# Order of two steps in the opening of a gated attention and expert-mix kernel: POOL's sums of x behind the low part of the score weights, a load of x behind a load of score weights

## The chip, the cores and the metric

The kernel runs on one core of a Trainium2 chip. Five engines work side by side, each through its own list of instructions in order, and wait for one another by semaphores: PE (matrix products), DVE and POOL (elementwise work and sums), ACT (copies, casts and functions such as exp), and SP, which here only issues DMA transfers. The metric is the device time of one execution in microseconds (us). Before the change it was 379.66 us, the median of three runs (379.59 to 382.38).

## The reference, cut to what matters

```python
g = sigmoid((x * gate_w).sum(-1, keepdims=True))
# a: linear attention with a learned feature map, 32 heads of 16
q, k, v = split_heads(x @ wqkv)
phi = lambda p: concat(softmax(p @ w_phi), softmax(-(p @ w_phi)))
kv, z = phi(k).T @ v, phi(k).sum(over tokens)
a = (phi(q) @ kv) / (phi(q) @ z + 1e-6) @ wo
# b: per token and head the best of 16 x 16 experts
s1, s2 = (x @ w_q)[first half] @ k1.T, (x @ w_q)[second half] @ k2.T
e = argmax(s1) * 16 + argmax(s2)
b = sum over heads of gelu(x . u[e]) * v[e]
return g * a + (1 - g) * b
```

x has 2048 rows of 512 numbers, so 16 tiles of 128 rows; all is float32.

## The kernel before, in words

A float32 product is made of three faster ones: each operand is split into a high part (a cast, written by ACT or DVE) and a low part (the rest, written by DVE or POOL), and PE adds high by high, high by low and low by high. So each operand has a pair of tiles: `xh` and `xl` for x, `sh` and `sl` for the score weights, `gh` and `gl` for sums of x.

The kernel has two large stages. The first (until about 118 us) reads x and makes the keys and values of all tiles, adds up `kv`, and beside that builds the score weights. The second goes over the 16 tiles once more for queries, scores and the output. The change lies in the first stage, which is written out by hand: the order of the lines is the order in which each engine gets its work.

Opening loop (lines 418 to 456), t = 0 to 4. For each t: keys of tile t (`kproj`, `k_diffs`, `k_exp`, `k_sum`, `k_mult`), one or more steps of `score`, and the split of a later tile of x (`x_split(t + 3)` at line 435).

Block-pair loop (lines 471 to 553), t = 5, 7, 9, 11, 13. Tiles t and n = t + 1 are taken together: their keys and values come from seven block products instead of eight (`prod`, line 461), which need sums and differences of the two raw tiles of x. The keys of tile n are finished in the next pass (`behind`). This text calls these passes "pass 5", "pass 7" and so on.

- `x_load(t)` (line 149): SP issues the DMA of a raw tile of x, 256 KB, into one of four buffers `xr`. In the opening loop, at lines 419 and 420, tile 7 is loaded at t = 1 and tile 8 at t = 2, ahead of the other work of that t. Tile 8 takes the buffer of tile 4, so its DMA waits until `x_split(4)` is done.
- `load_wq()` (line 143, called from `score`, line 406): SP issues the DMA of a block of `w_q`, 1 MB, into one of two buffers `st`. Block 4 takes the buffer of block 2, so its DMA waits until PE has used block 2 (`score_w`, line 299).
- `score` (line 400): PE multiplies a block of `w_q` by the keys k1 or k2 (`score_w`). After two blocks, `score_planes` (line 302) has ACT copy the result out of PSUM as 16-bit halves (`wpl`, line 304) and SP issue a DMA transposition of it (`wtp`, line 306).
- `join_tp` (line 314) has ACT put the transposed halves together again in the one buffer `wtj`; `join_end` (line 318) has ACT cast this to `sh` (line 321) and POOL write the rest to `sl` (line 322). Since `wtj` has one buffer, the next `join_tp` waits for that POOL instruction.
- `Sums.add(t)` (lines 172 to 178): four POOL instructions that replace raw tiles t and t + 1 by their sums and differences in place. They wait until the raw tiles have been split (`x_low`, line 156, on DVE). `Sums.high` (ACT, line 183) and `Sums.low` (POOL or DVE, line 189) split these sums for the products of the next pass.

In pass 5 POOL's list is: `Sums.add(7)`, the `sl` of column block 1 (`join_end(j1, tj1)`, line 500), `k_mult(4)` (line 516), the `sl` of column block 2 (from `join_all`, line 517), two small memsets, `Sums.low(7)`, `k_mult(5)`. ACT's list in pass 5 is: copy `pu` (489), `wtj` 1 (496), `wpl` 2 (497), `sh` 1, copy `pv` (512), exp of tile 4 (514), `wtj` 2, `sh` 2, `wpl` 3 (from `score`), `v` (531), exp of tile 5 (532), copy `pk` (536), and then `Sums.high(7)`. PE's last products of pass 5 (line 543) need that copy `pk`.

## Time and profile before

| | |
|---|---|
| median of three runs | 379.66 us (379.59 to 382.38) |
| the profiled execution, its time | 379.46 us |
| its span, first to last instruction | 376.8 us |
| granted PE clock, mean over the span | 0.994 |
| busy share of PE, DVE, ACT, POOL | 97%, 88%, 67%, 54% |
| wq loads, median from issue to landing | 6.2 us, 1024 KB each, 16 of them |
| transpositions `wtp`, median from issue to landing | 6.3 us, 8 of them |

In the views quoted below, times are us from the span's start. A timeline row has start, length, engine, line of the kernel, operation and tiles; a bracket gives the idle time of the engine before it and what ended that. The chain of work is followed back from the last instruction and lists, in order of time, what each moment waited for. A wait is a pair of who waited and for whom, with total, count and longest. A stretch gives the busy time of each engine between two times, the granted clock, and the DMA's share and rate. Lines of DMA issues give the queue, the count, the size and the time from issue to landing.

### The profile page before, as it was taken

How to read it: one execution, taken by the hardware profiler on the slowest of the kernel's cores; microseconds unless marked ns; L12 is line 12 of the kernel's file. 1: busy time of each engine (PE TensorE's matmuls, PEld its weight loads, DVE VectorE, ACT ScalarE, POOL GpSimd, SP SyncE). 2: the span in 40 equal slices, each digit the busy share in tenths (PEclk: the TensorE clock that was granted, in tenths of full speed). 3: DMA queues.
4: the chain of work that ended last, by engine and by line, in shares of the span. 5: the costliest groups of instructions: out<-in, count | busy, mean ns of one | idle time of the engine just before them, and what ended most of it. 6: DMA issues, size and time to landing. Idle time of an engine off the chain costs nothing.

```text
span 376.8 us, 8980 instructions
## 1 busy us (share of the span) xinstructions
PE 366.5 (97%) x3519; PEld 289.0 (77%) x3519; DVE 332.3 (88%) x783; ACT 253.0 (67%) x449; POOL 203.9 (54%) x205
## 2 busy tenths in 40 slices
PE   7999996999999999999999999999999999999996
PEld 3766675778778888878888888888888888888775
DVE  4679886999968889999999999899999999999993
ACT  4585657766766454879668678686686686687741
POOL 1089987698838726646427436344454454464700
PEclk9999998999999999999999999999999999999999
DMA  7867995359665032363342461453532532623201
GB/s 264 323 237 257 223 324 184 145 193 298 231 178 83 3 86 83 59 99 81 75 97 66 90 98 46 85 110 31 113 67 68 118 61 67 128 52 76 68 32 56
DMA packets 72219, 46.67 MB, mean 124 GB/s; under 512 B 63601, under 2 KB 64497, under 8 KB 69873
## 3 DMA queue, kind: packets, MB, share of 16 engines
q1 hardware_dynamic: 71312, 45.24, 45.8%
q10 hardware_dynamic: 864, 0.87, 0.8%
q8 instruction: 27, 0.44, 0.5%
q14 instruction: 16, 0.12, 0.1%
HBM read 26.43 MB, written 4.19 MB: 81 GB/s over the span
## 4 chain that ended last, share of the span: by engine, by line
PE 85%; DVE 4%; POOL 3%; ACT 3%; issue 2%; DMA 2%; SPq 0%; POOLq 0%; ACTq 0%; DVEq 0%
PE po L863 11%; PE s L56 8%; PE s L57 8%; PE s L58 8%; PE po L870 5%; PE pk L461 5%; PE pq L56 5%; PE pq L58 4%; PE pq L57 4%; PE pu L461 3%; PE oT L751 3%; PE pp L57 2%; PE pp L58 2%; PE pp L56 2%; PE ws L299 2%; PE kvacc L283 2%
## 5 line engine op out<-in xcount | busy, mean ns | idle before, releaser
L665 POOL TENSOR_TENSOR w<-d,zb 128x512 f32<-128x512 f32 x32 | 41.2, 1305 | 78.1 <-ACT d L659 78.1
L56 PE MATMUL s<-sh,xh 128*128 128x512 f32 x128 | 50.9, 398 | 0.0
L57 PE MATMUL s<-sl,xh 128*128 128x512 f32 x128 | 49.9, 390 | 0.0
L58 PE MATMUL s<-sh,xl 128*128 128x512 f32 x128 | 49.8, 389 | 0.0
L700 POOL TENSOR_TENSOR d<-d,st 128x512 f32<-128x512 f32 x30 | 31.2, 1063 | 27.7 <-DVE st L694 25.5
L659 ACT ACTIVATE d<-d 128x512 f32<-128x512 f32 x32 | 20.1, 632 | 34.7 <-DVE d L119 26.6
L276 POOL TENSOR_TENSOR d<-d,st 128x1024 f32<-128x1024 f32 x16 | 33.9, 2117 | 14.3 <-ACT d L267 10.0
L742 ACT COPY pt<-tp 128x1024 uint16<-128x1024 uint16 x28 | 36.3, 1364 | 0.0
L732 ACT COPY pl<-d 128x1024 uint16<-128x1024 uint16 x28 | 29.2, 1044 | 6.7 <-POOL d L700 6.7
L58 PEld LDWEIGHTS s<-sh,xl 128*128 128x128 f32 x128 | 24.0, 188 | 5.1
L56 PEld LDWEIGHTS s<-sh,xh 128*128 128x128 f32 x128 | 24.0, 188 | 4.7
L57 PEld LDWEIGHTS s<-sl,xh 128*128 128x128 f32 x128 | 24.1, 188 | 4.6
L56 PE MATMUL pq<-wah,xh 128*128 128x512 f32 x64 | 26.8, 418 | 0.0
L271 DVE TENSOR_REDUCE st<-d 128x64 f32<-128x1024 f32 x16 | 19.5, 1216 | 8.1 <-ACT d L267 7.7
L58 PE MATMUL pq<-wah,xl 128*128 128x512 f32 x64 | 25.1, 392 | 0.0
L57 PE MATMUL pq<-wal,xh 128*128 128x512 f32 x64 | 25.0, 390 | 0.0
L669 DVE TENSOR_REDUCE st<-d 128x32 f32<-128x512 f32 x32 | 21.6, 682 | 1.9 <-ACT d L659 0.4
L709 DVE TENSOR_TENSOR eq<-s,mx 128x512 bf16<-128x512 f32 x32 | 22.1, 691 | 1.2
L708 DVE TENSOR_REDUCE mx<-s 128x32 f32<-128x512 f32 x32 | 21.7, 680 | 0.0
L156 DVE TENSOR_TENSOR xl<-xr,xh 128x512 fp32r<-128x512 f32 (+2 forms) x17 | 19.1, 1149 | 1.8 <-ACT xh L152 1.6
L679 DVE TENSOR_REDUCE st<-w 128x32 f32<-128x512 f32 x32 | 20.4, 675 | 0.1
L267 ACT ACTIVATE d<-d 128x1024 f32<-128x1024 f32 x16 | 17.0, 1064 | 3.5 <-DVE d L121 3.5
(253 smaller groups left out, 1117.2 us busy)
## 6 DMA issues: line engine op xcount, KB each, us to landing
wq<-wq SPq DMA_DIRECT2D x16, 1024.0 KB, 6.2
xr<-xT SPq DMA_DIRECT2D x15, 256.0 KB, 4.7
y<-ot SPq DMA_DIRECT2D x15, 256.0 KB, 2.4
rawk<-wkT SPq DMA_DIRECT2D x1, 1024.0 KB, 6.6
rawq<-wqT SPq DMA_DIRECT2D x1, 1024.0 KB, 7.1
rawo<-wo SPq DMA_DIRECT2D x4, 256.0 KB, 3.6
rawu<-ug SPq DMA_DIRECT2D x2, 258.0 KB, 3.7
rawv<-wv ACTq DMA_DIRECT2D x2, 256.0 KB, 4.6
```

The source lines that it names most:

```text
L56: pe.matmul(o, ah, bh, start=(first and i == 0), stop=False)
L57: pe.matmul(o, ah, bl, start=False, stop=False)
L58: pe.matmul(o, al, bh, start=False, stop=(last and i == n - 1))
L276: pool.tensor_tensor(g64(d), g64(d), b64(st[:, 128:192]), op=ALU.mult)
L461: pe.matmul(o, x_, w_, start=(first and i + j == 0), stop=(i == 1 and j == 2), skip_group_check=True)
L665: pool.tensor_tensor(hs(e["w"], i), hs(e["ph"], i), hs(zb, i), op=ALU.mult)
L700: eng.tensor_tensor(g64(d)[:, gs_], g64(d)[:, gs_], r[:, gs_].unsqueeze(2).to_broadcast([P, 32, F]), op=ALU.mult)
L708: dve.tensor_reduce(mx, p3, axis=AX.X, op=ALU.max)
L709: dve.tensor_tensor(e["eq"][:, 512 * half:512 * half + 512].rearrange("p (h f) -> p h f", f=F), p3, mx.unsqueeze(2).to_broadcast([P, H, F] ...
L732: act.copy(pl, e["ph"][:, halves[i]].bitcast(U16).rearrange("p (c j) -> p j c", j=2))
L742: act.copy(p16[:, :, 4 * i:4 * i + 4, :], e["tp"][i].rearrange("p (j g) n -> p j g n", j=2))
L863: pe.matmul(po, a, b, start=(i == 0), stop=False)
```

## The change

In the opening loop the loads of tiles 7 and 8 of x move from the head of the pass (t = 1 and t = 2) to behind `x_split(t + 3)`. On SP's list that puts them behind what that pass's `score` issues: at t = 1 `score` issues nothing, at t = 2 it issues the load of block 4 of `w_q`. In pass 5 `Sums.add(7)` moves from ahead of the join of column block 1 to behind its `join_end`. Passes 7, 9 and 11 keep `Sums.add` where it was, and pass 13 had none.

```diff
     for t in range(5):
-        if t in (1, 2):
-            x_load(t + 6)
         if t > 2:
             vproj(t)()
         kproj(t)
...
         if t < 3:
             x_split(t + 3)
+        if t in (1, 2):
+            x_load(t + 6)
         if t == 2:
             x_split(6)
             Sums.add(5)
...
         prod(a, tile_of(t, 0), b11, True)
         b = mm_bank(f"pu{t}")
         act.copy(b, a)
-        if t + 3 < NT:
+        if 5 < t < NT - 3:
             Sums.add(t + 2)
         if t == 5:
             (j1, tp), = joins
...
             load_wq()
             load_wq()
             join_end(j1, tj1)
+            Sums.add(t + 2)
         elif t < NT - 3:
             join_all()
```

## The prediction, on record before the result

> **What bounds the kernel now.** I read the page first, then the list of waits of PE, then the chain of work around the one long wait, then the granted clock there, and at last the lists of POOL, ACT, DVE and SP in the same place. PE is busy nearly throughout:

> ```profile
> PE 366.5 (97%) x3519; PEld 289.0 (77%) x3519; DVE 332.3 (88%) x783; ACT 253.0 (67%) x449; POOL 203.9 (54%) x205
> ```

> So time can be won only where PE waits or runs slowly. Its list of waits has two entries that lie in the part of the kernel that the change touches:

> ```profile
> PE pk L461 <- ACT pk L536: 3.0, 1, 3.0
> PE ws L299 <- DMA wq<-wq: 0.9, 1, 0.9
> ```

> The chain of work shows what stands behind the 3.0 us (start, length, what):

> ```profile
> 54.40 0.55 POOL xr L178
> 55.09 1.30 POOL sl L322
> 56.41 1.38 ACT wtj L315
> ...
> 59.84 0.96 ACT d L267
> 60.80 0.50 ACT pk L536
> 61.34 4.61 PE pk L461 x12
> ```

> Backwards: PE's last products of pass 5 wait for ACT's copy `pk`; ACT had been working without a break since its second join `wtj` at 56.41; that join waits for POOL's first `sl`, because `wtj` has one buffer; and POOL's `sl` stands behind `Sums.add(7)`, whose last instruction is the first row. Three stretches show what the waits do to the clock (us, then busy time of PE, PEld, DVE, ACT, POOL, then the granted clock):

> ```profile
> 44.00:45.10 1.10, 0.19 (x6) 0.01 (x3) 1.10 (x3) 0.17 (x1) 1.02 (x3) 1.00 0.31 74
> 58.54:61.95 3.41, 0.61 (x3) 0.52 (x4) 1.12 (x1) 3.41 (x6) 1.43 (x4) 1.00 0.66 163
> 61.95:65.37 3.42, 3.42 (x10) 2.65 (x9) 3.28 (x6) 1.43 (x3) 3.42 (x3) 0.50 0.28 77
> ```

> After 0.9 us without work the clock stays at 1.00. After the 3.0 us it is 0.50 for 3.4 us. So the long wait costs twice: 3.0 us idle, and then twelve products that take 4.61 us from 61.34. The same twelve in the next pass, and the chain after them:

> ```profile
> 76.01 2.72 PE pk L461 x12
> 78.73 1.36 PE pe L461 x6
> 80.09 1.36 PE pu L461 x6
> ```

> They take 2.72 us there; with 0.1 us for the restart the slow clock costs 4.61 - 2.82 = 1.8 us.

> **The change part by part.** *The sums behind the `sl`.* ACT's list has the cast that `sl` needs, and the join that waits:

> ```profile
> 50.95 0.64 ACT L321 CAST sh<-wtj 128x512 fp32r<-128x512 f32 x1
> ...
> 56.41 1.38 ACT L315 COPY wtj<-wtp 128x1024 uint16<-128x1024 uint16 x1 [3.35 <-POOL sl L322]
> ```

> and POOL's list in passes 5 and 7:

> ```profile
> 51.95 0.74 POOL L175 TENSOR_TENSOR xr<-xr 128x256 f32<-128x256 f32 x1 [1.41 <-DVE xl L156]
> ...
> 56.34 1.94 POOL L276 TENSOR_TENSOR d<-d,st 128x1024 f32<-128x1024 f32 x1
> ...
> 61.90 1.29 POOL L189 TENSOR_TENSOR gl<-xr,gh 128x512 fp32r<-128x512 f32 x1 [1.98 <-ACT gh L183]
> ...
> 76.51 1.32 POOL L189 TENSOR_TENSOR gl<-xr,gh 128x512 fp32r<-128x512 f32 x1
> 77.78 1.75 POOL L189 TENSOR_TENSOR xl<-xr,xh 128x512 fp32r<-128x512 f32 x1
> ```

> The cast `sh` is done at 51.59 and POOL is idle until 51.95. So `sl` can run from about 51.6 to 53.0 instead of 55.09 to 56.39: 3.4 us earlier. The four sums then start at 53.0, 1.05 us later than before, take the same 55.09 - 51.95 = 3.1 us and end at 56.1. Behind them stands `k_mult(4)`, which began at 56.34 and so loses nothing. The sums are next needed by ACT's `gh` cast at about 60, nearly 4 us on: the move itself costs nothing.

> ACT's join doesn't gain the whole 3.4 us. It also needs its input, the transposition that SP issues after ACT's copy `wpl`. The issue, and the landing counted from it (a second row is the longest landing of such a transposition, that of 73.02):

> ```profile
> 51.09 1.24 SPq L306 DMA_TRANSPOSE wtp<-wpl  x1
> wtp<-wpl SPq DMA_TRANSPOSE x1, 3.9
> wtp<-wpl SPq DMA_TRANSPOSE x1, 8.4
> ```

> 51.09 + 3.9 = 55.0, and nothing in the change moves that. So the join starts at about 55.06 instead of 56.41: 1.35 us earlier, and the transposition is late next. What follows on ACT up to `pk` must be ready 1.35 us earlier too: its last input is DVE's `d` of tile 5, done at 57.23 and needed at 59.84 - 1.35 = 58.49. DVE's rows:

> ```profile
> 56.55 0.68 DVE L121 TENSOR_TENSOR d<-st,pk 128x512 f32<-128x512 f32 x1
> ...
> 70.16 0.69 DVE L115 TENSOR_REDUCE st<-pk 128x32 f32<-128x512 f32 x1 [0.44 <-PE pk L461]
> ```

> So PE resumes at 59.99, and its wait is 1.65 us instead of 3.0.

> *The clock.* No row shows a wait of 1.65 us. The ends are 0 (as after 0.9 us) and 1.8 us (as after 3.0 us). 1.65 is nearer to 0.9, and the stretch after which the clock fell had 0.61 of 3.41 us busy, while a stretch of that length with the shorter wait in it has at least 1.76 busy, half of it. I take 1.8 us won. [...]

> *What takes part of it back.* With both, PE is 1.35 + 1.8 = 3.15 us ahead in pass 7. DVE isn't: it starts pass 7 only 1.35 us earlier, behind ACT, and wins 0.44 more where it waited for PE at 70.16, so 1.79 us. POOL's `gl` and `xl` for pass 9 hang on DVE through `k_mult(6)` and come 1.79 us earlier: 77.83 becomes 76.04 and 79.53 becomes 77.74. PE would want `gl` at 78.73 - 3.15 = 75.58, waits to 76.04, takes 1.36 us, and waits from 77.40 to 77.74 for `xl`. That product began at 80.09, so 80.09 - 77.74 = 2.35 us remain. From there all engines are about 2.3 us early and the old slack is back, so I carry 2.35 us to the end.

> *The loads of x.* At t = 1 nothing is issued on SP between the old place and the new one: no effect. At t = 2 one DMA of 256 KB moves behind one of 1 MB. SP, the landings, PE and ACT:

> ```profile
> 33.08 0.33 SPq L149 DMA_DIRECT2D xr<-xT  x1
> 33.50 0.38 SPq L143 DMA_DIRECT2D wq<-wq  x1
> ```

> ```profile
> wq<-wq SPq DMA_DIRECT2D x1, 1024.0 KB, 4.9
> xr<-xT SPq DMA_DIRECT2D x1, 256.0 KB, 2.6
> ```

> ```profile
> 29.21 1.07 PE L299 MATMUL ws<-wq,kp 128*32 128x512 f32 x8
> ```

> ```profile
> 40.03 1.15 ACT L152 CAST xh<-xr 128x512 fp32r<-128x512 f32 x2
> ```

> The block of `w_q` waits only for PE's use of its buffer, done at 30.28, so it can go at 30.3 and land near 35.2. Tile 8 still waits for its own buffer until 33.08; if it even had to queue behind the whole of the other, it lands at 35.2 + 2.6 = 37.8. ACT casts tiles 7 and 8 from 40.03 on. So the cost is 0 to both sides of these bounds. A gain could come only from the 0.9 us wait for block 5, by an emptier DMA; that block's own issue stays, since it waits for PE, so I take 0 (ends 0 and 0.9).

> The sum: 1.35 + 1.8 - 0.8 = 2.35 us. The profiled execution took 379.46 us, 0.2 below the median of 379.66; its span is 376.8. From the median, 379.66 - 2.35 = 377.3 us.

> **The rivals.** *The clock falls anyway.* A wait of 1.65 us may suffice. Then the 1.8 us stay lost, DVE keeps up, and the gain is 1.35 us: 378.3 us. For it: no row between 0.9 and 3.0 us. Against it: half of the stretch is work.

> *The wait for `w_q` goes as well.* If the earlier block 4 clears the DMA for block 5, PE and with it ACT's `wpl` and the transposition come 0.9 us earlier: 3.25 us won, 376.4 us. Against it: block 5 is issued when PE frees its buffer, as before.

> *The transposition lands late (slower).* It is now what ACT waits for. The old order hid any landing up to 56.4, which is 5.3 us after its issue; from there on it costs. With the longest landing, 8.4 us, the join would start at 59.5 instead of 56.41, 3.1 us later: 382.8 us. Against it: that one was issued right behind two loads of `w_q`, and in pass 5 these come after it on SP.

> *Nothing happens.* If some other input of ACT's run from 56.41 to 61.30 is as late as the join was, the gain is 0: 379.7 us. The `d` row speaks against it.

> **How the numbers follow.** My forecast, 377.3 us, has 0.62; the clock rival 0.18; the `w_q` rival 0.08; the late transposition 0.06; nothing 0.06. The range from 376.2 to 378.6 holds the first three, with 0.2 us for the spread of medians. One per cent, about what a measurement of this kernel can tell from no change, is 3.8 us: below 375.9 only with the `w_q` wait gone and nothing given back (1.35 + 1.8 + 0.9 = 4.05 us), 0.03; above 383.5 only with a landing over 9 us, 0.03; within, 0.94.

> **What would show it.** Right: POOL's first `sl` in pass 5 starts near 51.6 and its sums near 53.0; ACT's second join starts near 55.1 with the transposition as releaser; PE's wait for `pk` is about 1.65 us; no stretch of clock 0.50 after it; small waits of PE for `gl` and `xl` in pass 9. SP issues the fifth block of `w_q` near 30.3 and tile 8 at 33.1, with the wait of 0.9 us unchanged. Wrong: clock 0.50 again near 63; a join that starts at 56 or later; a changed wait for `w_q`; or PE still 3.15 us ahead after pass 9.

## The result, and the profile after

The changed kernel takes 376.55 us, the median of eight runs (375.40 to 377.66). The kernel before has 380.89 us over the eight runs that now stand beside it (379.59 to 382.50). The ratio is 0.9885 with a 95% interval of 0.9855 to 0.9916, so 4.4 us are won (3.2 to 5.5). The forecast was 2.35 us. That its 377.3 us lies within 0.8 us of the measured time is luck in part: its base, 379.66 us from three runs, was 1.2 us under the later median, from which the same 2.35 us would have given 378.5 us. Two executions of the experiments below, of 1449.81 and 721.47 us, lie far outside all others and are left out of every median and ratio.

The profiled execution took 375.40 us and spans 373.6 us; the one before took 379.46 and spanned 376.8. PE's list of waits, where 3.0 us for `pk` and 0.9 us for `w_q` stood before:

```profile
PE pk L461 <- ACT pk L537: 1.6, 1, 1.6
```

No entry for `w_q` is left. The chain of work of the changed kernel shows the shorter wait and the twelve products after it, which took 4.61 us before:

```profile
57.56 1.07 ACT d L267
58.63 0.50 ACT pk L537
...
59.17 3.03 PE pk L461 x12
62.20 1.36 PE pe L461 x6
```

PE resumes at 59.17 instead of 61.34, and the products run at full clock. Two stretches around the wait (same columns as in the prediction; the clock is the third number from the end):

```profile
55.80:59.21 3.41, 1.79 (x9) 1.15 (x7) 1.92 (x4) 3.41 (x6) 3.41 (x3) 1.00 0.97 379
59.21:62.62 3.41, 3.41 (x15) 2.82 (x16) 3.27 (x5) 2.39 (x5) 3.36 (x6) 1.00 0.81 106
```

ACT's second join and, on POOL, the first `sl` and the first of the four sums behind it (its bracket names the load of x, but DVE's low parts, shown in the last section, end later, at 53.13):

```profile
54.26 1.36 ACT L315 COPY wtj<-wtp 128x1024 uint16<-128x1024 uint16 x1 [1.99 <-DMA wtp<-wpl]
```

```profile
50.88 1.71 POOL L322 TENSOR_TENSOR sl<-wtj,sh 128x512 fp32r<-128x512 f32 x1 [0.16 <-ACT sh L321]
53.21 0.73 POOL L175 TENSOR_TENSOR xr<-xr 128x256 f32<-128x256 f32 x1 [0.63 <-DMA xr<-xT]
```

The join waits for the transposition now, and no longer for POOL. But it starts at 54.26, not at 55.06: the transposition itself was issued at 50.59 and landed 3.6 us later, where it had been 51.09 and 3.9 us. The loads of x did what the lists said and no more. SP issues block 4 of `w_q` at 30.50 and tile 8 at 33.22, as against 33.50 and 33.08:

```profile
30.50 0.33 SPq L143 DMA_DIRECT2D wq<-wq  x1
33.22 0.33 SPq L149 DMA_DIRECT2D xr<-xT  x1
```

### The profile page after: what moved, and what is told of

Its sections match the earlier page's. It is cut to its first block, busy times and chain, and to the rows that moved or that the text cites. A ratio compares the mean times of both kernels' runs of the same rounds, so it can differ in the third digit from the quotient of the medians.

```text
span 373.6 us, 8981 instructions
## 1 busy us (share of the span) xinstructions
PE 366.0 (98%) x3519; PEld 287.6 (77%) x3519; DVE 333.6 (89%) x783; ACT 252.8 (68%) x449; POOL 205.3 (55%) x205
## 4 chain that ended last, share of the span: by engine, by line
PE 95%; DMA 1%; POOL 1%; ACT 1%; issue 1%; DVE 0%; ACTq 0%; POOLq 0%
PE po L864 11%; PE s L56 8%; PE s L58 8%; PE s L57 8%; PE po L871 6%; PE pk L461 5%; PE pq L56 5%; PE ws L299 4%; PE pq L58 4%; PE pq L57 4%; PE pu L461 4%; PE oT L752 3%; PE kvacc L283 3%; PE pp L57 2%; PE pp L58 2%; PE pp L56 2%
## 5 line engine op out<-in xcount | busy, mean ns | idle before, releaser
L276 POOL TENSOR_TENSOR d<-d,st 128x1024 f32<-128x1024 f32 x16 | 33.6, 2102 | 13.3 <-DVE st L272 10.8
L156 DVE TENSOR_TENSOR xl<-xr,xh 128x512 fp32r<-128x512 f32 (+2 forms) x17 | 20.5, 1232 | 1.5 <-ACT xh L152 1.4
L267 ACT ACTIVATE d<-d 128x1024 f32<-128x1024 f32 x16 | 17.0, 1063 | 5.2 <-DVE d L121 5.2
## 6 DMA issues: line engine op xcount, KB each, us to landing
wq<-wq SPq DMA_DIRECT2D x16, 1024.0 KB, 6.2
xr<-xT SPq DMA_DIRECT2D x15, 256.0 KB, 3.9
y<-ot SPq DMA_DIRECT2D x15, 256.0 KB, 2.5
rawk<-wkT SPq DMA_DIRECT2D x1, 1024.0 KB, 6.4
rawq<-wqT SPq DMA_DIRECT2D x1, 1024.0 KB, 6.3
rawo<-wo SPq DMA_DIRECT2D x4, 256.0 KB, 3.9
rawv<-wv ACTq DMA_DIRECT2D x2, 256.0 KB, 4.8
```

The costliest lines, as they stand in the source:

```text
L276: pool.tensor_tensor(g64(d), g64(d), b64(st[:, 128:192]), op=ALU.mult)
```

## The experiments

The theory: the move of the sums carries the whole result, by the earlier join and by the clock that isn't lost; the loads carry nothing, and the wait for `w_q` was a chance of the profiled execution before. The main rival: the loads removed that wait and so carry 0.9 us or more.

**The change again** (`e0_change`, no edit).

> The changed kernel once more, as a measure for its two halves on the same chip. The profile of the change showed PE's wait for pk at 1.6 us instead of 3.0, no stretch at clock 0.50, and no wait for w_q. If these three explain the result, this run is 3.2 to 4.1 us under the kernel before and shows the first two again; whether the wait for w_q (0.9 us before) is absent again tells if it goes with the change or with the execution.

376.50 us beside 380.32 us of the kernel before, ratio 0.9900 (0.9871 to 0.9929): 3.8 us won. PE waits 1.4 us for `pk`, not at all for `w_q`, and the clock is 1.00.

**The sums alone** (`e1_sums_only`).

```diff
-        if t + 3 < NT:
+        if 5 < t < NT - 3:
             Sums.add(t + 2)
...
             join_end(j1, tj1)
+            Sums.add(t + 2)
```

> Only POOL's sums behind the sl; the loads of x stay where they were. Theory: this half carries the result, by the earlier join on ACT (1.35 us) and the kept clock (1.8 us), so 2.4 to 3.2 us under the kernel before, PE's wait for pk about 1.6 us, clock 1.00 throughout, and the wait for w_q still 0.9 us. Rival: the loads carry part; then the join starts near 55.1 (change: 54.3) and this run is 0.8 us or more above the whole change.

375.52 us, ratio 0.9884 (0.9858 to 0.9911): 4.4 us won, as much as by the whole change. The wait for `pk` is 1.7 us and the clock 1.00. The wait for `w_q`, which the theory left at 0.9 us, is absent here too, with the loads in their old order. So is the rival's sign: the join starts at 53.92, not near 55.1.

**The loads alone** (`e2_loads_only`).

```diff
     for t in range(5):
-        if t in (1, 2):
-            x_load(t + 6)
...
         if t < 3:
             x_split(t + 3)
+        if t in (1, 2):
+            x_load(t + 6)
```

> Only the loads of tiles 7 and 8 behind the split; the sums stay ahead of the sl. Theory: worth nothing, since the sl still ends near 56.4 behind the sums, whose start hangs on DVE's splits; time within 0.5 us of the kernel before, clock 0.50 for 3.4 us again; if the wait for w_q goes, PE's wait for pk grows by as much (3.0 to 3.9 us). Rival: the emptier DMA is worth its 0.9 us by itself, 0.9 us under the kernel before.

380.38 us, ratio 1.0004 (0.9978 to 1.0029): nothing. Its profile shows where an earlier PE goes when the join still waits for POOL. The wait for `w_q` is down to 0.2 us, and PE's wait for `pk` is 3.7 us instead of 3.0:

```profile
56.71 1.35 ACT L315 COPY wtj<-wtp 128x1024 uint16<-128x1024 uint16 x1 [4.10 <-POOL sl L322]
```

The transposition landed at 50.65 + 3.7 = 54.35 in this execution, but the join started at 56.71. So the old order hid 2.4 us of it and not 1.35. The clock fell again:

```profile
57.64:61.05 3.41, 0.26 (x2) 0.00 (x0) 0.00 (x0) 3.38 (x6) 2.33 (x4) 1.00 0.42 155
61.06:64.47 3.41, 2.86 (x7) 2.29 (x8) 3.23 (x5) 2.59 (x6) 2.30 (x2) 0.50 0.35 67
```

**The kernel before with work in the wait** (`e3_fill_before`). The ten products multiply zeros into a bank that is overwritten right after.

```diff
+        prod(c, sums(1, 2), b22, False)
         d = pks[n] = mm_bank(f"pk{n}")
+        if t == 5:
+            for _ in range(10):
+                pe.matmul(d[:, :384], warm[:, 1:P + 1], warm[:, :384], start=True, stop=True)
         act.copy(d, b)
-        prod(c, sums(1, 2), b22, False)
```

> The kernel before with ten additional products of zeros (128x384, their result overwritten) ahead of PE's long wait, so that PE has work in part of the 3.0 us; the wait's end doesn't move. It isolates the clock. Theory: the clock stays at 1.00, the twelve products after the wait take 2.8 instead of 4.6 us, and of these 1.8 us 1.0 to 1.5 are left at the end, since DVE and POOL are no earlier and PE then waits for them in pass 9. Rival: the slow stretch is no loss because DVE sets the pace there; then the time is that of the kernel before within 0.3 us.

378.28 us, ratio 0.9949 (0.9928 to 0.9970): 1.9 us won (1.1 to 2.7) without moving the end of the wait. That is what the filling wins through the clock, on average over its executions. The chain shows the twelve products at 3.01 us, and in pass 9 a hold-up: from the start of the next twelve to that pass's `ws` products it takes 81.50 - 74.24 = 7.26 us.

```profile
61.21 3.01 PE pk L461 x12
...
74.24 2.72 PE pk L461 x12
...
81.50 1.85 PE ws L299 x16
```

In the kernel before the twelve began at 76.01 and the `ws` products here, which is 6.80 us:

```profile
82.81 1.85 PE ws L299 x16
```

The mean granted clock of every execution is on record, and one stretch of 3.41 us at 0.50 takes 0.0045 from it (3.41 x 0.5 / 376.8). It is at most 0.996 in all 56 executions of the kernel before that stand beside the experiments, and at least 0.997 in 17 of 19 of the change. The filled kernel kept the clock in 7 of its 12 executions; their median is 377.77 us, that of the other five (0.994 or 0.995) 379.05. So within one kernel a lost clock goes with 1.3 us.

The other 2.5 us of the sums alone (4.4 less 1.9) are put down to the earlier join. By subtraction that is uncertain by more than 1 us, but the profiles agree: both kernels have the old loads and no wait for `w_q`, and the join starts at 56.31 in the filled one and at 53.92 in the sums alone, 2.4 us earlier.

**Key differences first** (`e4_kd_first`, on the changed kernel).

```diff
+        if behind:
+            k_diffs(behind)
         for u in (t + 2, t + 3):
             if u < NT - 1:
                 x_low(u)
-        if behind:
-            k_diffs(behind)
```

> The change, and in passes 7 to 13 DVE's key differences of the tile left over go ahead of the low parts of x. In the changed kernel those two low parts took 3.5 us beside POOL's multiplication, and PE was held up by about 0.4 us in pass 9. Theory: DVE no longer stands behind POOL there, PE's hold-up in pass 9 goes and 0.4 us are won over the change (4.2 to 4.6 us under the kernel before). Rival: the sums of pass 7, which wait for the low parts, come later and hold up PE instead: equal to the change or above it.

377.29 us, ratio 0.9911 (0.9877 to 0.9946). This overlaps the change's interval and settles nothing about 0.4 us. Its profile is of use all the same: the transposition landed 4.2 us after its issue, PE waited 2.2 us, and the clock fell.

```profile
55.70:59.11 3.41, 1.26 (x6) 0.71 (x4) 1.47 (x3) 3.41 (x6) 3.41 (x5) 1.00 1.31 379
59.12:62.53 3.41, 3.35 (x8) 2.68 (x9) 2.88 (x5) 2.10 (x5) 2.88 (x5) 0.50 0.68 67
```

**Copy of pk first** (`e5_pk_first`, on the changed kernel).

```diff
-        k_exp(t)
-        k_sum(t)
+        if t > 5:
+            k_exp(t)
+            k_sum(t)
         prod(b, sums(0, 0), b3, False)
         d = pks[n] = mm_bank(f"pk{n}")
         act.copy(d, b)
+        if t == 5:
+            k_exp(t)
+            k_sum(t)
```

> The change, and in pass 5 ACT copies pk ahead of the exp of tile 5. PE's wait for pk shrinks from 1.4 to 1.6 us to about 0.5. Theory: DVE and POOL, which hang on that exp, come 0.6 us later and PE gives the gain back in pass 9: within 0.4 us of the change. Rival: PE is the bound alone: 0.9 us under the change.

376.04 us, ratio 0.9884 (0.9857 to 0.9910): no difference from the change that these runs can show. PE's waits for `pk` fell to 0.7 us for the long one (1.1 for two), and the chain then runs through DVE's low parts and POOL's `gl` to PE in pass 9. So what PE won was given back to DVE and POOL, as far as the chain shows it.

**Both edits** (`e6_both`).

> Both edits together on the change. Theory: with DVE's delay gone the shorter wait for pk is kept, 0.9 to 1.3 us under the change (5 to 5.5 us under the kernel before). Rival: something else of pass 7 or 9 is the next bound and it stays within 0.4 us of the change.

374.34 us, ratio 0.9849 (0.9821 to 0.9877): 5.7 us under the kernel before (4.7 to 6.8). By the medians that is about 2 us under the change. The wait for `pk` is 0.6 us, and pass 9 takes 77.74 - 70.94 = 6.80 us again, without a hold-up:

```profile
57.88 3.01 PE pk L461 x12
...
70.94 2.72 PE pk L461 x12
...
77.74 1.85 PE ws L299 x16
```

**Loads of w_q ahead of the transposition** (`e7_loads_ahead`, on the changed kernel).

```diff
-            score_planes(2)
             load_wq()
             load_wq()
+            score_planes(2)
```

> The change, but SP issues the two loads of w_q of pass 5 ahead of the transposition, which then stands behind 2 MB. It tests that the transposition is what ACT's second join waits for after the change. Theory: the join starts at 58 to 59.5 instead of 54.2, PE's wait for pk is 6 us or more, the clock is 0.50 for 3.4 us again, and the time is 5 to 7 us above the change, so 1 to 3 us above the kernel before. Rival: the join has another input as late as the transposition; then the time stays within 1 us of the change.

386.37 us, ratio 1.0145 (1.0109 to 1.0181): 5.5 us above the kernel before, more than the 1 to 3 us expected. The join starts even later than expected, at 60.82 and not at 58 to 59.5 us, when the transposition has landed:

```profile
60.82 1.33 ACT L315 COPY wtj<-wtp 128x1024 uint16<-128x1024 uint16 x1 [9.15 <-DMA wtp<-wpl]
```

```profile
PE pk L461 <- ACT pk L537: 9.4, 2, 8.6
```

So the transposition is what the join waits for. The time is more than expected also because the clock stayed at 0.50 for three stretches of 3.41 us, from 59.27 to 69.50, where one was forecast: the mean clock is 0.987, and the twelve products after the wait take 4.78 us from 65.69. The rival of a late transposition was a real danger, which this change by itself doesn't meet.

**A late block of w_q, with the old and the new order of the sums** (`e8_late5_before`, `e9_late5_change`, on the kernel before and on the changed one). After these runs one point was open: why the join gained 2.4 us and not 1.35. Both kernels get the same edit in `score`.

```diff
-            if not 4 < done < 9:
+            if not 3 < done < 9:
                 load_wq()
             if planes and done % 2 == 0:
                 score_planes(done // 2 - 1)
+            if done == 4:
+                load_wq()
```

> The kernel before, with SP's load of block 5 of w_q moved behind the transposition of the opening loop (issue about 41.6 instead of 37 us). It forces a wait of PE for w_q near 44 us, of about 4 us, where the profiled execution before had 0.9 by chance. Theory: such a wait delays ACT's wpl and the transposition but not POOL's sums, so the transposition lands near 59 and the old order of the sums costs nothing any more: the join is released by the transposition, and this run equals its twin with the new order within 1 us, both 1 to 3 us above the kernel before. Rival: the old order costs its 2.5 us whatever is late ahead of it, and the twins stay 2 us or more apart.

> The twin of the late block 5, on the changed kernel: the same move of the load, the sums behind the sl. Theory: the join is released by the transposition near 59 us and the time equals that of the twin with the old order within 1 us, so the gain of the change is gone; 4 to 6 us above the change. Rival: 2 us or more below the twin.

378.73 us with the old order, 378.90 us with the new one; ratios 0.9957 (0.9933 to 0.9982) and 0.9948 (0.9926 to 0.9969). The order of the sums is worth nothing that these runs can show once PE waits 2.8 us for block 5. ACT's joins in the two, old order first:

```profile
57.48 1.36 ACT L315 COPY wtj<-wtp 128x1024 uint16<-128x1024 uint16 x1 [1.17 <-DMA wtp<-wpl]
```

```profile
57.52 1.37 ACT L315 COPY wtj<-wtp 128x1024 uint16<-128x1024 uint16 x1 [1.20 <-DMA wtp<-wpl]
```

Both wait for the transposition, issued at 54.35 and 54.36. In both profiles the clock is lost at the wait for `w_q` instead, 0.50 for 3.41 us from 47.60 and from 47.20, and the twelve products after the wait for `pk` take 3.04 and 3.02 us; so the order has no clock to win there either. I had the level wrong: both are under the kernel before (1.6 us for the old order), not 1 to 3 us above it. The two waits of PE are 2.8 us for `w_q` and only 0.8 us for `pk`, 3.6 us together, as long as the 3.7 us of the loads alone; the profiles give no more than 0.5 us of the difference (spans of 376.7 and 377.2 us), and the rest I can't place. The clock may be part of it: 4 of 11 executions with the old order and 3 of 11 with the new one kept it (mean 1.00), and none of the 12 of the loads alone (at most 0.995).

**Both edits and the change side by side** (`e10_both_again`, `e11_change_again`).

> The change with both further edits (key differences first, copy of pk first) once more, in one call with the change, to compare the two on the same chip. Theory: 1 to 2 us under the change. Rival: the earlier distance came from the chip or the call, and the two are within 0.5 us.

> The change once more, beside the kernel with both further edits and the twins with the late block 5. Theory: 3.8 to 4.4 us under the kernel before, and no wait of PE for w_q in its profile.

374.50 us, ratio 0.9836 (0.9806 to 0.9866), and 376.77 us, ratio 0.9899 (0.9862 to 0.9936). The version with both further edits is 2.3 us under the change by the medians, as it was about 2 us under it before; its slowest execution (375.06) is faster than the fastest of the change (375.59). It beats both kernels: 6.2 us under the kernel before (5.1 to 7.4).

## Why the prediction was right in kind and short in size

The place, the mechanism and the sign were right: POOL's `sl` at 50.88, its sums at 53.21, the join released by the transposition, full clock after the wait for `pk`, and loads that are worth nothing. That this wait is 1.6 us, with 1.65 forecast, is luck in part: PE resumed 2.17 us earlier, not 1.35, but it had also come to the wait 0.8 us earlier. The sums have 2.6 us to spare (they end at 56.41, and ACT reads them at 59.04), not nearly 4, which is enough. The gain of 4.4 us (3.2 to 5.5) leaves the forecast 2.35 outside its interval. Step by step:

- **The join (forecast 1.35 us): mis-sized, about 2.4 us.** The step that failed is "51.09 + 3.9 = 55.0, and nothing in the change moves that". In the execution I read, PE had waited 0.9 us for `w_q` at 44.2, which held up ACT's copy `pu`, and behind it `wpl` and the transposition. The `sl` of that execution was not held up, since its sums hang on DVE (it starts at 55.09, and at 55.38 in the loads alone). So the profile showed a distance of 1.35 us that is 2.4 us when the wait for `w_q` is absent, as in the loads alone (54.35 against 56.71). The filled kernel and the sums alone, both without that wait, show 2.4 us too (56.31 against 53.92), the times put the join at 4.4 - 1.9 = 2.5 us, and the twins show the same thing from the other side: with a longer wait for `w_q` the distance is gone.
- **The wait for `w_q` (forecast unchanged, 0.9 us).** It is gone, or 0.2 us in the loads alone, in the profile of the change and in those of all experiments but the two that force it. The kernel before had block 5 landing 8.0 us after its issue, the change 7.1; with the loads in their old order the sums alone and the filled kernel have no wait for `w_q` either, so nothing shows that it goes with the loads. Why the landing varies was not tried. A changed wait was one of the prediction's own signs of being wrong, and its rival with this wait gone (3.25 us won, 376.4 us) came nearer than the forecast; but the rival's cause, the loads, is not it: the loads alone show 0.
- **The clock (forecast 1.8 us): right in kind, a little less in size.** At full clock the twelve products take 3.03 us after a wait, 0.3 us more than the 2.72 without one, where the forecast allowed 0.1, an estimate; so the profiles show 4.61 - 3.03 = 1.6 us. Filling the wait alone wins 1.9 us (1.1 to 2.7), after what pass 9 gives back. That the clock would hold was forecast by the work in the stretch, and this is what told the cases apart (last section), with little to spare: one of the first eight executions of the change has a mean clock of 0.994.
- **What is given back (forecast 0.8 us): half of it.** In the change pass 9 takes 79.48 - 72.26 = 7.22 us instead of 6.80, so 0.4 us. The mechanism was right: the copy of `pk` first won nothing alone and paid together with the key differences first. The chain of the change stops in pass 9, at POOL's `gl` and `xl`:

```profile
70.86 1.40 PE pv L461 x6
...
73.94 1.23 POOL gl L189
75.17 1.71 POOL xl L189
...
76.92 1.19 PE pu L461 x4
78.11 1.37 PE pk L461 x6
79.48 1.85 PE ws L299 x16
```

  The size failed because I had PE want `gl` and `xl` at the first product of each group; only the third one reads them, 0.45 us later. With the prediction's own times, that alone leaves 0.35 us of the 0.8.

- **The loads (forecast 0): right**, 1.0004 (0.9978 to 1.0029).

With the sizes that the profiles show the sum is 2.4 + 1.6 (4.61 less 3.03 for the twelve products) - 0.4 = 3.6 us, inside the interval of 3.2 to 5.5.

Left open: executions of one kernel differ by some us (378.8 to 382.5 for the kernel before, 375.3 to 377.7 for the change), and the profiled execution before spent 379.46 - 376.8 = 2.7 us outside its span where that of the change spent 1.8. The wait for `w_q` may be part of the first; no run here shows the rest.

## What to carry to other kernels

Where a one-buffer tile makes one engine wait for another, look at what stands ahead of the releasing instruction on that engine's list; four sums that nobody needed for another 6 us (they ended at 55.1, and ACT read them at 61.2) cost about 2.4 us by standing there, and through the clock between 1 and 2 us more. Before the distance to the next-late input is taken as the gain, ask whether that input was itself late by a chance of this one execution. And a wait removed in one pass is kept only if the other engines of the next passes are early too: here a still shorter wait for `pk` paid only together with a second reordering on DVE.

## What the runs showed of the hardware that I had not expected

```profile
56.88:60.29 3.41, 1.85 (x11) 0.90 (x10) 0.00 (x0) 3.38 (x5) 2.70 (x4) 1.00 0.54 214
```

In the filled kernel the boundary at 60.29 split the wait of 2.5 us, which ended at 61.21; with the key differences first the wait of 2.2 us ended at 59.18, and the boundary was at 59.11. The stretches are equally long throughout the two traces of before and after: in the kernel before, 17 of 3.413 us lie between 3.93, where the record begins at 1.00, and its fall at 61.95, and 91 between its return at 65.37 and its fall at 375.98, at the end of the work; in the change 108 lie between 4.60 and 373.24. The boundaries lie differently in each execution (58.54 before, 55.80 in the change, 57.64 with the loads alone). The executions of one kernel differ as well: the filled kernel, whose profile has the wait of 2.5 us, kept the clock in 7 of 12, and of the seven with the key differences first, whose profile has the wait of 2.2 us, four have a mean clock of 0.994 or 0.995 and three of 0.999 or 1.000. That the place of the boundary decides this is my estimate from these cases; no run sets the place.

A second thing: with POOL's `sl` started beside them, DVE's two low parts in pass 5 took 2.38 us, and held up the sums behind the `sl` to 53.21. The row of the change, and that of the kernel before:

```profile
50.75 2.38 DVE L156 TENSOR_TENSOR xl<-xr,xh 128x512 fp32r<-128x512 f32 x2
```

```profile
50.59 1.28 DVE L156 TENSOR_TENSOR xl<-xr,xh 128x512 fp32r<-128x512 f32 x2
```

Nothing further was held up: POOL's next multiplication starts at 56.35, where it had started at 56.34. The experiments show the same: in the repeat of the change and in the sums alone the `sl` starts at 50.91 and 50.53, beside the two low parts, and these take 2.38 and 2.40 us; in the loads alone and in the filled kernel it starts only at 55.38 and 54.98, and they take 1.29 us in both. What in the hardware makes them slower was not shown.
